# Value rows loaded in five transfers a pair with 96-key runs, and two table halves negated on VectorE

## The chip, the cores and the metric

The kernel runs on one core of one Trainium2 chip. The metric is the device time in microseconds (us) of one execution, as the median of several runs. The core has five instruction streams that matter here: TensorE (PE, with its weight loads shown as PEld), VectorE (DVE), ScalarE (ACT), GpSimd (POOL) and SyncE (SP). SP, ACT and POOL can each issue DMA transfers, and 16 DMA engines move the data.

## What is computed

Chunked attention, then a Fourier mix, a layer norm and a two-layer MLP. Shapes: q, k and v are (4 batches, 8 heads, 768, 64) in float32, with 8 memory keys and values for each head; x is (4, 768, 512); the MLP is 512 to 2048 to 512.

```
for c in range(24):                          # chunks of 32 queries
    keys  = 8 memory keys + k[32*c-16 : 32*c+40]    # 16 left, 32 own, 8 right, cut at the ends
    a     = softmax(q_c @ keys.T / 8)
    out_c = a @ values
x   = heads side by side
u   = x + real(fft(fft(x, axis=1), axis=2))
un  = (u - mean) / sqrt(var + 1e-6)
out = u + max(un @ w_ch1, 0) @ w_ch2
```

## The kernel before

**Pairs and tiles.** The 32 heads are taken as 16 pairs, n = 0 to 15, four pairs for each batch (`HP` = 4). The 768 positions of a head are cut into `NT` = 12 tiles of 64 queries (two chunks). For each tile, scores are computed with the keys on the partitions: partitions 0 to 7 hold the memory keys, 8 to 23 the 16 left keys, 24 to 87 the 64 own keys, 88 to 95 the 8 right keys. `OWN` is 24 and `KEYS` is 96. Neighbouring tiles overlap, so the value buffer `va` ([128 partitions, 2 heads, 12 tiles, 66], float32) holds each value row more than once; column 64 of a row is 1, so that the softmax's denominator comes out of the same product. There are four such buffers (`NV` = 4), so pair n uses buffer n % 4.

**Value loads** (`e_load_v`, lines 386 to 406). For one pair: one transfer for the own rows of tile 0 of both heads (line 399), and for each head one of left and own rows of tiles 1 to 11 (80 partitions x 11 tiles, line 392), one of right rows of tiles 0 to 10 (8 partitions x 11 tiles, also line 392), and one that repeats the 8 memory values for 12 tiles (line 405). That is seven transfers, whose pieces are rows of 64 floats, 256 bytes. All are issued by SP, except that in batch 0 the 80-row transfer of the second head is issued by ACT (`half == 1`).

**Edges.** The left rows of tile 0 and the right rows of tile 11 do not exist. They are set to 0 once for each buffer, with their column 64 (`e_edges`, lines 351 to 355, and `e_edge_ones`, lines 357 to 365), by GpSimd except for buffer 0. `e_masks` (lines 339 to 345) makes the bias `mbias` that takes out, for the first chunk of a tile, keys 64 to 95, and for the second chunk the keys ahead of its left context.

**Keys and products.** `e_kT` (line 450) spreads the turned keys over `kTb` with 88 columns for each tile (11 blocks of 8). `e_scores` (line 464) and `a_scores` make the scores `sc`; `e_exp` (line 475) and `a_exp` write `e1` on `KEYS` partitions; `e_values` (line 511, matmul at line 523) multiplies `e1[0:KEYS]` with `va[0:KEYS]` into `xa` (tiles 0 to 5) and `xo` (tiles 6 to 11); `e_norm` (line 527) divides.

**Fourier tables.** In batch 0 the sequence transform takes its rows in two halves (`g_rows`, line 719, matmul at line 729); the second half needs `odd`, the negative of one parity of the cosine and sine tables. `e_negatives` (line 1232, instruction at line 1234) makes it on GpSimd, two instructions on 128 x 579 float16.

**Order.** Each engine follows a list of task numbers written out by hand (`lists`, from line 1597). The planner (`Plan.order`) plays the lists through with a cost for each task, and from that decides in which overall order the instructions are emitted, which of two PSUM banks a task gets, and how many filler matmuls (`e_fill`, line 1040) PE runs where the planner has it idle in the first part of the kernel. Task 113 is the negation. It stands in GpSimd's list behind the q load of pair 2 and ahead of the last edge tasks and the q and k loads of pair 3 (tasks 88 and 89). A GpSimd copy of one value (`e_gate`, line 1121) reads a row of pair 3's second head; behind it in GpSimd's list stand the q and k loads of pairs 4 and 5 and the first two weight loads.

Of the kernel before, what the change touches and what calls it, by code (L numbers as in the profile page):

```python
# [16 lines left out]
CHUNK = 32  # L17
# [5 lines left out]
OWN = MEM0 + NMEM + LEFT  # L23
KEYS = OWN + 2 * CHUNK + RIGHT

# [183 lines left out]
def kernel(  # L209
# [129 lines left out]
    def e_masks():  # L339
        nc.gpsimd.memset(mbias, 0.0)  # L340
        nc.gpsimd.memset(mbias[64:96, 0:1], NEG)
        nc.gpsimd.affine_select(out=mbias[:, 1:2], in_=mbias[:, 1:2], compare_op=ALU.is_ge,
                                fill=NEG, base=-(OWN - LEFT + CHUNK), pattern=[[0, 1]],
                                channel_multiplier=1)
        nc.gpsimd.memset(mbias[MEM0:MEM0 + NMEM, 1:2], 0.0)
# [5 lines left out]
    def e_edges(i):  # L351
        v1, eng = va[i], nc.vector if i < 1 else nc.gpsimd
        eng.memset(v1[:, :, :, D:D + 1], 1.0)  # L353
        eng.memset(v1[0:32, :, 0, 0:D], 0.0)
        eng.memset(v1[64:96, :, NT - 1, 0:D], 0.0)

    def e_edge_ones(i):
        v1 = va[i]
        lo, hi = v1[0:32, :, 0, D:D + 1], v1[64:96, :, NT - 1, D:D + 1]
        nc.gpsimd.affine_select(out=lo, in_=lo, compare_op=ALU.is_ge, fill=0.0, base=-OWN,  # L360
                                pattern=[[0, 2], [0, 1]], channel_multiplier=1)
        nc.gpsimd.affine_select(out=hi, in_=hi, compare_op=ALU.is_ge, fill=0.0,
                                base=OWN + 63 - 64, pattern=[[0, 2], [0, 1]],
                                channel_multiplier=-1)
        nc.gpsimd.memset(v1[MEM0:MEM0 + NMEM, :, 0, D:D + 1], 1.0)
# [20 lines left out]
    def e_load_v(n, half=None):  # L386
# [3 lines left out]
        def run(p0, count, t0, nt, key, hh, by):  # L390
# [3 lines left out]
                                      ap=[[D, count], [64 * D, nt], [1, D]]))  # L394

        if half == 1:
            run(OWN - LEFT, LEFT + 64, 1, NT - 1, 64 - LEFT, 1, nc.scalar)
            return
        nc.sync.dma_start(v1[OWN:OWN + 64, :, 0, 0:D],
                          v[b, 2 * pr:2 * pr + 2, 0:64].rearrange("h p d -> p h d"))  # L400
        for hh in range(2):
            if half is None or hh == 0:
                run(OWN - LEFT, LEFT + 64, 1, NT - 1, 64 - LEFT, hh, nc.sync)
            run(OWN + 64, RIGHT, 0, NT - 1, 64, hh, nc.sync)
            nc.sync.dma_start(v1[MEM0:MEM0 + NMEM, hh, :, 0:D],
                              mem_v[b, 2 * pr + hh].unsqueeze(1).to_broadcast([NMEM, NT, D]))
# [43 lines left out]
    def e_kT(n, eng=None):  # L450
        if n >= TURNED * HP:
            win = LEFT + 64 + RIGHT
            nc.vector.tensor_copy(
# [4 lines left out]
        (eng or nc.scalar.copy)(  # L458
            strided(kTb[n % NKT], MEM0 + NMEM, [[P, NT], [RB, 11], [1, RB]]),
            strided(trk, 0, [[64 // RB, NT], [1, 11], [KP, RB]]))  # L460
        if n < 2 or n in JOINED:
# [49 lines left out]
    def e_values(n, g):  # L511
# [6 lines left out]
        for st in range(3):  # L518
            for hh in range(2):
                v1 = va[n % NV]  # L520
                for half in range(2):
                    t6 = 2 * st + half
                    nc.tensor.matmul(xa[64 * half:64 * half + 64, st, hh, 0:65],  # L523
                                     e1[0:KEYS, hh, t6, :], v1[0:KEYS, hh, 6 * g + t6, 0:65],
                                     start=True, stop=True)
# [706 lines left out]
    def e_negatives():  # L1232
        for i, tab in enumerate((cosS, sinS)):
            nc.gpsimd.tensor_scalar(odd[:, i], tab[:, 1], -1.0, None, ALU.mult)

# [22 lines left out]
    t_warm = add("ACT", 1.6, lambda: nc.scalar.activation(warm, zero, AFT.Exp), [t_late], rank=LATER)  # L1258
    t_neg = shared(add("POOL", 3.3, e_negatives, [t_sines], rank=100))
    t_rows = shared(add("POOL", 2.8, e_table_rows, [t_late, t_neg], rank=LATER))  # L1260
# [330 lines left out]
    for b in range(B):  # L1591
# [6 lines left out]
        "DVE": [  # L1598
# [18 lines left out]
        ],  # L1617
# [34 lines left out]
        "POOL": [  # L1652
# [4 lines left out]
        ],  # L1657
# [40 lines left out]
```

## Time and profile before

| | us |
|---|---|
| median of 3 runs | 272.72 |
| lowest, highest | 272.63, 278.22 |
| the profiled execution | 271.1 |
| its span in the profile | 269.4 |

The profiled execution's own time is 1.7 us above its span. TensorE's granted clock was 1.0 in it.

A row of a timeline gives the start in us, the duration in us, the engine, the line, the operation with what it writes and reads, the number of instructions merged, and in brackets how long the engine had been idle and what released it. A row of the chain of waits gives start, duration and what held the chain; "DMA" there is the time from a transfer's issue to its landing, "SPq" the issuing of a transfer on SP. A row of the DMA view gives a queue's packets, megabytes and the time of its packets as a share of 16 engines' time: q1 is SP's queue, q10 ACT's, and q0 ("software") GpSimd's. In the lists of groups the last numbers are total busy us and mean ns of one instruction.

### The profile page before, as it was taken

To read this page: it belongs to the slowest core of one execution; us is meant where nothing else is said; L and a number is where in the kernel's file an instruction comes from. 1 tells how busy PE (TensorE), PEld (TensorE's weight loads), DVE (VectorE), ACT (ScalarE), POOL (GpSimd) and SP (SyncE) were. 2 spreads that over 40 slices of the span, in tenths; PEclk is the share of its full clock that TensorE was granted. 3 is DMA by queue.
4 is the path that set the end of the run, shared out by engine and by line. 5 is a ranking of instruction groups with operands and counts; after the bars stand their busy time and mean duration, and the time that the engine had idled before them with its cause. 6 is when DMAs were issued, how large, how long until landed. Compare 5 with 4: busy or idle time off the path is not lost.

```text
span 269.4 us, 8363 instructions
## 1 busy us (share of the span) xinstructions
PE 260.8 (97%) x3469; PEld 215.8 (80%) x3469; DVE 202.7 (75%) x456; ACT 162.8 (60%) x318; POOL 89.6 (33%) x159
## 2 busy tenths in 40 slices
PE   6999899999999999999899999999999999999995
PEld 6556597888964778857798888888988988888884
DVE  6867488863379779999999989999887855354444
ACT  6757868899866279766742974726627171715150
POOL 7985463045120091564480550006006231000000
PEclk9999999999999999999999999999999999999999
DMA  6999999979998999989999974681913233334263
GB/s 102 206 180 191 211 195 200 213 126 195 197 241 169 130 218 175 126 222 206 197 218 161 159 169 88 165 130 19 238 20 82 61 77 80 89 61 108 56 166 92
DMA packets 116118, 40.00 MB, mean 148 GB/s; under 512 B 104560, under 2 KB 111472, under 8 KB 116080
## 3 DMA queue, kind: packets, MB, share of 16 engines
q1 hardware_dynamic: 90304, 22.64, 46.5%
q0 software_dynamic: 21472, 15.21, 34.8%
q10 hardware_dynamic: 4304, 1.62, 3.0%
q8 instruction: 27, 0.44, 0.7%
q14 instruction: 11, 0.09, 0.1%
HBM read 37.36 MB, written 13.37 MB: 188 GB/s over the span
## 4 chain that ended last, share of the span: by engine, by line
PE 73%; DVE 11%; DMA 8%; POOL 4%; issue 1%; SPq 1%; ACT 0%; POOLq 0%
PE ph L908 27%; PE pc L975 21%; PE pc L926 5%; PE ps L595 5%; DMA va<-in_v_dram 5%; DMA va<-in_mem_v_dram 3%; PE xa L523 3%; PE xo L523 3%; PE ps L729 2%; PE pm L768 2%; DVE st L843 1%; DVE xsb L534 1%; PE pm L789 1%; DVE xsb L817 1%; PE sc L494 1%
## 5 line engine op out<-in xcount | busy, mean ns | idle before, releaser
L908 PE MATMUL ph<-unT,w_sb 128*128 128x256 f16 x768 | 88.9, 273 | 0.2 <-DVE xsb L980 0.2
L917 ACT ACTIVATE hT<-ph 128x512 f16<-128x512 f32 x96 | 55.2, 600 | 51.6 <-PE pc L975 37.5
L908 PEld LDWEIGHTS <-w_sb 128*128 128x128 f16 x768 | 74.2, 98 | 9.7 <-issue 0.5
L975 PEld LDWEIGHTS <-hT 128*128 128x128 f16 x360 | 34.6, 98 | 4.5 <-DVE hT L963 0.2
L975 PE MATMUL pc<-w_sb,hT 128*128 128x256 f16 x288 | 36.6, 273 | 0.0
L980 DVE TENSOR_TENSOR xsb<-pc,xsb 128x256 f32<-128x256 f32 x64 | 26.1, 419 | 13.7 <-PE pc L975 12.8
L831 POOL TENSOR_TENSOR xsb<-mix,xr 128x512 f32<-128x512 f32 x9 | 12.3, 1384 | 42.3 <-ACT mix L825 24.4
L506 ACT ACTIVATE e<-sc,mbias 96x192 f32<-96x192 f32 (+1 forms) x48 | 19.0, 470 | 5.0 <-PE sc L494 5.0
L926 PE MATMUL pc<-w_sb,hT 128*128 128x512 f16 x96 | 21.7, 379 | 0.0
L481 ACT ACTIVATE e<-sc,mbias 96x384 f32<-96x384 f32 x32 | 17.0, 573 | 6.8 <-PE sc L471 6.8
L963 DVE TENSOR_TENSOR S<-hT 128x768 f16<-128x768 f16 (+1 forms) x18 | 7.6, 421 | 17.2 <-ACT hT L917 16.9
L857 ACT ACTIVATE un<-xsb,rs 128x512 f16<-128x512 f32 x18 | 14.4, 821 | 5.3 <-POOL rs L872 5.3
L975 PE MATMUL pc<-w_t,S 128*128 128x256 f16 x144 | 17.4, 273 | 0.0
L926 PEld LDWEIGHTS <-hT 128*128 128x128 f16 x96 | 9.1, 98 | 10.1
L843 DVE BATCH_NORM_STATS2 st<-xsb 128x6 f32<-128x512 f32 x24 | 16.3, 681 | 0.8 <-POOL xsb L831 0.6
L523 PE MATMUL xa<-va,e 96*64 96x65 f32 x384 | 14.9, 226 | 1.3 <-DMA va<-in_mem_v_dram 1.3
L523 PEld LDWEIGHTS xa<-va,e 96*64 96x64 f32 x384 | 12.6, 137 | 3.7 <-issue 2.9
L975 PEld LDWEIGHTS <-S 128*128 128x128 f16 x144 | 14.0, 98 | 1.6
L523 PE MATMUL xo<-va,e 96*64 96x65 f32 x384 | 14.1, 223 | 0.0
L1040 PE MATMUL idle<-dz 128*128 128x512 bf16 x46 | 12.9, 387 | 1.0 <-DVE va L353 1.0
L433 ACT COPY qT<-trq 128x768 bf16<-128x768 bf16 x12 | 9.6, 796 | 6.6 <-PE trq L415 6.4
L523 PEld LDWEIGHTS xo<-va,e 96*64 96x64 f32 x384 | 12.6, 138 | 0.4 <-ACT e L481 0.2
(192 smaller groups left out, 489.1 us busy)
## 6 DMA issues: line engine op xcount, KB each, us to landing
va<-in_v_dram SPq DMA_DIRECT2D x28, 220.0 KB
w_sb<-in_moe_w_ch_dram POOLq DMA_DIRECT2D x8, 512.0 KB, 9.0
out_dram<-xsb SPq DMA_DIRECT2D x12, 256.0 KB
qs<-in_q_dram POOLq DMA_DIRECT2D x12, 192.0 KB, 6.7
ks<-in_k_dram POOLq DMA_DIRECT2D x12, 192.0 KB, 6.6
x_rows<-xsb POOLq DMA_DIRECT2D x3, 768.0 KB, 5.1
xr<-x_back POOLq DMA_DIRECT2D x3, 768.0 KB, 5.7
out_rows<-xsb SPq DMA_DIRECT2D x9, 256.0 KB
```

The source lines that it names most:

```text
L481: nc.scalar.activation(e1[0:KEYS, :, :, ts(half, 32)], sc[0:KEYS, :, 0:6, ts(half, 32)], AFT.Exp, bias=mbias[0:KEYS, half:half + 1], scale ...
L506: nc.scalar.activation(to, src, AFT.Exp, bias=mbias[0:KEYS, half:half + 1], scale=1.0 / math.sqrt(D))
L523: nc.tensor.matmul(xa[64 * half:64 * half + 64, st, hh, 0:65], e1[0:KEYS, hh, t6, :], v1[0:KEYS, hh, 6 * g + t6, 0:65], start=True, stop=True)
L595: nc.tensor.matmul(out_[:, sp, :], part[:, ab, sp * 3 + st, c0:c1], tab[:, sp, st, :], start=(st == 0 and i == 0), stop=(st == 2 and i == 1))
L843: nc.vector.bn_stats(st6, xs[b][:, kt, :])
L857: nc.scalar.activation(un, xs[b][:, kt, :], AFT.Identity, bias=rs[:, 1:2], scale=rs[:, 0:1])
L908: nc.tensor.matmul(ph[:, k, :], w1_sb[:, dt, ts(HH * k + i, P)], unT_of[b, j][:, dt, :], start=(dt == 0), stop=(dt == NDT - 1))
L917: nc.scalar.activation(hT_of[b, j][:, :, i, :], ph, AFT.Relu, bias=0.0, scale=1.0 if (b, j) in FAST else -1.0)
L926: nc.tensor.matmul(pc_of[b, j, r], hT_of[b, j][:, k, i, ts(r, P)], w2_sb[:, HH * k + i, :], start=(i + k == 0), stop=(i + k == HH))
L975: nc.tensor.matmul(pc_of[key], a[:, i, :], w[:, i, :], start=(i == 0 and new), stop=(i == HH - 1), skip_group_check=not new)
L980: nc.vector.tensor_tensor(u, pc, u, ALU.add)
L1040: nc.tensor.matmul(fill_of[0], dz, strided(dz, 0, [[0, 4], [1, P]]), start=True, stop=True)
```

## The change

The keys of a tile are followed by 16 rows instead of 8 (`AFTER` = 16), so that `KEYS` grows from 96 to 104. Right rows then need no transfer of their own: left, own and following rows of a tile are one run of 96 consecutive keys. For each head that is one transfer of 96 partitions x 11 tiles, and tile 0 of both heads takes one of 80 rows; with the two of memory values a pair has five transfers. The run of tile 11 reads 16 rows into the next head, which the last tile's product leaves out (it uses `LAST` = 88 rows); only for the very last head, where there is no next, the run is split into two transfers. The mask takes out keys 64 to 103 for the first chunk and 96 to 103 for the second. The edge memsets and selects for tile 11 go. `e_kT` spreads 96 columns a tile instead of 88. Task 113 moves from GpSimd to VectorE, with a planned cost of 0.5 us instead of 3.3, behind task 69 (the norm of pair 1's second half) and ahead of task 116 (the first Fourier fold). The other numbers in the lists keep their order.

```diff
-KEYS = OWN + 2 * CHUNK + RIGHT
+AFTER = 2 * RIGHT
+LAST = OWN + 2 * CHUNK
+KEYS = LAST + AFTER
...
-        nc.gpsimd.memset(mbias[64:96, 0:1], NEG)
+        nc.gpsimd.memset(mbias[64:P, 0:1], NEG)
+        nc.gpsimd.memset(mbias[96:P, 1:2], NEG)
...
         eng.memset(v1[0:32, :, 0, 0:D], 0.0)
-        eng.memset(v1[64:96, :, NT - 1, 0:D], 0.0)
...
-        lo, hi = v1[0:32, :, 0, D:D + 1], v1[64:96, :, NT - 1, D:D + 1]
+        lo = v1[0:32, :, 0, D:D + 1]
...
-        nc.gpsimd.affine_select(out=hi, in_=hi, compare_op=ALU.is_ge, fill=0.0,
-                                base=OWN + 63 - 64, pattern=[[0, 2], [0, 1]],
-                                channel_multiplier=-1)
...
+        def rows(hh, by):
+            whole = (b, 2 * pr + hh) != (B - 1, H - 1)
+            run(OWN - LEFT, KEYS - OWN + LEFT, 1, NT - 2 + whole, 64 - LEFT, hh, by)
+            if not whole:
+                run(OWN - LEFT, LEFT + 64, NT - 1, 1, S - 64 - LEFT, hh, by)
+
         if half == 1:
-            run(OWN - LEFT, LEFT + 64, 1, NT - 1, 64 - LEFT, 1, nc.scalar)
+            rows(1, nc.scalar)
             return
-        nc.sync.dma_start(v1[OWN:OWN + 64, :, 0, 0:D],
-                          v[b, 2 * pr:2 * pr + 2, 0:64].rearrange("h p d -> p h d"))
+        nc.sync.dma_start(v1[OWN:KEYS, :, 0, 0:D],
+                          v[b, 2 * pr:2 * pr + 2, 0:64 + AFTER].rearrange("h p d -> p h d"))
         for hh in range(2):
             if half is None or hh == 0:
-                run(OWN - LEFT, LEFT + 64, 1, NT - 1, 64 - LEFT, hh, nc.sync)
-            run(OWN + 64, RIGHT, 0, NT - 1, 64, hh, nc.sync)
+                rows(hh, nc.sync)
...
-            strided(kTb[n % NKT], MEM0 + NMEM, [[P, NT], [RB, 11], [1, RB]]),
-            strided(trk, 0, [[64 // RB, NT], [1, 11], [KP, RB]]))
+            strided(kTb[n % NKT], MEM0 + NMEM, [[P, NT], [RB, 12], [1, RB]]),
+            strided(trk, 0, [[64 // RB, NT], [1, 12], [KP, RB]]))
...
+                    rows = LAST if 6 * g + t6 == NT - 1 else KEYS
                     nc.tensor.matmul(xa[64 * half:64 * half + 64, st, hh, 0:65],
-                                     e1[0:KEYS, hh, t6, :], v1[0:KEYS, hh, 6 * g + t6, 0:65],
+                                     e1[0:rows, hh, t6, :], v1[0:rows, hh, 6 * g + t6, 0:65],
...
-            nc.gpsimd.tensor_scalar(odd[:, i], tab[:, 1], -1.0, None, ALU.mult)
+            nc.vector.tensor_scalar(odd[:, i], tab[:, 1], -1.0, None, ALU.mult)
...
-    t_neg = shared(add("POOL", 3.3, e_negatives, [t_sines], rank=100))
+    t_neg = shared(add("DVE", 0.5, e_negatives, [t_sines], rank=100))
...
-            30, 69, 116, 31, 120, 115, 92, 119, 83, 87, 123, 100, 129, 134, 104, 132, 138, 137, 142, 141, 227,
+            69, 113, 116, 31, 120, 115, 92, 119, 83, 87, 123, 100, 129, 134, 104, 132, 138, 137, 142, 141, 227, 144,
...
-            36, 2, 11, 37, 55, 54, 13, 15, 18, 71, 9, 8, 19, 12, 70, 113, 10, 14, 88, 89, 32, 91, 208, 207,
+            36, 2, 11, 37, 55, 54, 13, 15, 18, 71, 9, 8, 19, 12, 70, 10, 14, 88, 89, 32, 91, 208, 207, 225, 224,
```

More of the change, by code (lines that the diff above doesn't have):

```diff
@@ L451, in e_kT @@
         if n >= TURNED * HP:
-            win = LEFT + 64 + RIGHT
+            win = LEFT + 64 + AFTER
             nc.vector.tensor_copy(
```

39 rows, old and new, of the table lists are left out of this document.

## The prediction, as made before the result was known

> **What bounds the kernel now.** I read the page first, then the chain of waits, then the stretch before 34 us in it, because there alone the chain is not on TensorE.
>
> ```profile
> PE 73%; DVE 11%; DMA 8%; POOL 4%; issue 1%; SPq 1%; ACT 0%; POOLq 0%
> ```
>
> TensorE holds 73% of the chain, so what counts is where it waits, and how much of its work is filler. Its waits after 33 us (us in all, times, longest):
>
> ```profile
> PE ps L595 <- ACT hT L917: 0.7, 1, 0.7
> PE pm L768 <- DVE up L757: 0.5, 1, 0.5
> PE ph L908 <- DVE xsb L980: 0.2, 1, 0.2
> ```
>
> Only 1.4 us in 236, and no transfer among them: a microsecond won on TensorE before 33 us should last to the end. The 8% of DMA lies before that. The chain there:
>
> ```profile
> 17.01 5.83 DMA va<-in_v_dram
> ...
> 22.85 0.27 SPq L392
> ...
> 23.16 9.32 DMA va<-in_mem_v_dram
> ```
>
> The last transfer of pair 3's values is issued at 23.16 and lands 9.32 us later; the value product of that pair has begun and stands still for it. On TensorE's timeline:
>
> ```profile
> 23.41 0.82 PE L1040 MATMUL idle<-dz 128*128 128x512 bf16 x3
> ...
> 30.95 0.34 PE L523 MATMUL xa<-va,e 96*64 96x65 f32 x4
> 32.62 0.80 PE L523 MATMUL xa<-va,e 96*64 96x65 f32 x20 [1.33 <-DMA va<-in_mem_v_dram]
> ...
> 34.46 0.92 PE L523 MATMUL xo<-va,e 96*64 96x65 f32 x24
> ```
>
> The undisturbed group takes 0.92; this one took from 30.95 to 32.62 + 0.80 = 33.42, so **the stall costs 33.42 - 30.95 - 0.92 = 1.55 us**.
>
> Why is that transfer late? Two things. First, SP issues late:
>
> ```profile
> 15.73 0.59 SPq L399 DMA_DIRECT2D va<-in_v_dram  x1
> 16.36 1.08 SPq L392 DMA_DIRECT2D va<-in_v_dram  x2
> 17.49 0.32 SPq L405 DMA_DIRECT2D va<-in_mem_v_dram  x1
> 17.96 0.27 SPq L392 DMA_DIRECT2D va<-in_v_dram  x1
> 18.28 0.31 SPq L405 DMA_DIRECT2D va<-in_mem_v_dram  x1
> 18.64 0.59 SPq L399 DMA_DIRECT2D va<-in_v_dram  x1
> 19.79 1.89 SPq L392 DMA_DIRECT2D va<-in_v_dram  x2
> 21.72 0.31 SPq L405 DMA_DIRECT2D va<-in_mem_v_dram  x1
> 22.85 0.27 SPq L392 DMA_DIRECT2D va<-in_v_dram  x1
> ```
>
> The chain hangs the one at 22.85 on the landing of the one of 17.01 (the second of the row of 16.36). Counting rows, it is the eighth after it, and buffers of different pairs are concerned. I read: a transfer from SP or ACT waits for the landing of the one eight places earlier, so eight are in flight, whatever their size. Second, GpSimd's loads then take the DMA engines. The DMA view of 20 to 24 us, then of 24 to 32 us:
>
> ```profile
> q1 hardware_dynamic: 1414, 0.35, 43.8%
> ```
> ```profile
> q0 software_dynamic: 882, 1.43, 101.4%
> q1 hardware_dynamic: 558, 0.13, 11.6%
> ```
>
> SP's queue falls from 1414 / 4 = 354 packets a us to 558 / 8 = 70. That flood begins behind GpSimd's gate, which waits for ACT's load of pair 3:
>
> ```profile
> 11.87 1.70 POOL L1234 TENSOR_SCALAR odd<-cosS 128x579 f16<-128x579 f16 x1
> 13.54 1.80 POOL L1234 TENSOR_SCALAR odd<-sinS 128x579 f16<-128x579 f16 x1
> ...
> 19.91 0.18 POOL L1121 COPY gate<-va 1x1 f32<-1x1 f32 x1 [0.38 <-DMA va<-in_v_dram]
> ```
>
> **The change, part by part.** *Transfers and packets.* A pair has 128 + 2 x (880 + 88 + 96) = 2256 pieces of 256 bytes before, and 160 + 2 x (1056 + 96) = 2464 after: 9% more. In batch 0, SP's share goes from 1376 to 1408, ACT's from 880 to 1056. But eight in flight are now 1.6 pairs instead of 1.1. Counting the new order, pair 2's first two wait for the end of pair 0 and the first transfer of pair 1 only, and the last transfer of pair 3 (memory values, second head) is the eighth after ACT's load of pair 3, the very one that opens the gate.
>
> *When pair 3 lands.* ACT's loads of pairs 1 to 3 have 3 x 176 = 528 more packets; at SP's lone rate of 354 a us that is 1.5 us, so the gate opens at about 19.9 + 1.5 = 21.4, and the flood reaches SP's queue at about 25.5 instead of 24. The last transfer is issued at about 21.4 too. Ahead of it stand at most pair 3's 1056-piece run and the other memory transfer: 1056 + 192 = 1248 packets, 3.5 us at 354. It lands near 25, and TensorE asks at 30.95. The slack is some 6 us, or 5.45 x 70 = 380 packets left over when the flood begins at 25.5. So the 1.55 us go. What is late next is the exponential of pair 3's second half, which its product reaches only behind twelve Fourier products (the 34.46 row above comes 34.46 - 33.42 = 1.04 after the first product's end), and then TensorE's own queue, which the three waits above show to be full: **-1.55 us**.
>
> By the Trainium skill, DMA: Bandwidth & Descriptors, section "Why a DMA increments its semaphore by 16 and not by 1", a transfer is spread over the largest number of engines up to 16 that divides its slowest dimension, which puts an 8-row transfer on 8 of the 16. By it the fuller engines would carry 2 x (55 + 11 + 12) + 8 = 164 pieces a pair before and 2 x (66 + 12) + 10 = 166 after, 1% more instead of 9%, and pair 3 would land earlier still; no row here names an engine.
>
> *The negation.* 1.70 + 1.80 = 3.5 us leave GpSimd. Behind it are the last edges and pair 3's q and k loads, which go some 3.5 us earlier; the gate does not, since it waits for a landing. VectorE gets two instructions of 579 float16 ahead of the first of these:
>
> ```profile
> 23.81 0.95 DVE L671 TENSOR_TENSOR half<-xsb 128x762 f32<-128x762 f32 x1
> ...
> 27.47 0.96 DVE L699 TENSOR_TENSOR lo<-half,hi 128x768 f16<-128x768 f32 x1 [1.04 <-ACT hi L695]
> ```
> ```profile
> L453 DVE COPY kTb<-kU 128x1056 bf16<-128x1056 bf16 x4 | 1.7, 420 | 0.0
> ```
> ```profile
> L671 DVE TENSOR_TENSOR half<-xsb 128x762 f32<-128x762 f32 x2 | 1.9, 949 | 0.1
> ```
>
> No row has this operation on VectorE. The low end is the 16-bit copy, 579 / 1056 x 420 = 0.23 each; the high end one float32 pass, 579 / 762 x 949 = 0.72 each. Nearest is the copy, one 16-bit source and no second operand: 0.5 for both, 1.4 at worst. Queued behind it are two folds, a small copy and the keys' constant columns, and then VectorE waits 1.04 us for ScalarE: 0.5 is hidden, of 1.4 some 0.4 would be left for whoever waits for that result. **0**, at worst +0.4.
>
> *Wider copies, more rows.* `e_kT` copies 12 columns of blocks instead of 11. The by-shape list has:
>
> ```profile
> L458 ACT COPY kTb<-trk 128x1056 bf16<-128x1056 bf16 x9 | 9.3, 1034 | 0.6 <-PE trk L415 0.6
> ```
> ```profile
> L415 PEld LDWEIGHTS <-qs 96*64 96x64 bf16 x192 | 5.1, 110 | 2.0 <-issue 1.6 <-DMA qs<-in_q_dram 0.4
> ...
> L415 PEld LDWEIGHTS <-ks 100*64 100x64 bf16 x192 | 5.0, 109 | 1.4 <-issue 1.3
> ```
>
> At most 1034 / 11 = 94 ns more for each of twelve, and TensorE's waits after 33 show the copies of later pairs in none: 0. The value product contracts 104 rows instead of 96: weight loads of 100 and 96 rows differ by 1 ns, so 0; the other bound is below, as a rival. The dropped edge memsets let pair 1's first load go a few tenths earlier, which the slack hides.
>
> *Filler.* The planner counted the negation as 3.3 us ahead of pair 3's loads. If it filled for these, as with the three fillers of 23.41 ahead of pair 3's turned q, up to 0.8 us of filler go; if it sees more competition among loads, as much may be added. I take 0.
>
> The sum: 271.1 - 1.55 = 269.5 for the profiled execution, and as the median of the runs lies 1.6 above that one, **272.72 - 1.55 = 271.2**.
>
> **The rivals.** *A: more filler goes.* -1.55 - 0.8 or somewhat more: 270.2. For it: fillers stand ahead of pair 3's q in the row of 23.41, and a filler runs whether the load has come or not; against it, no row shows what the planner saw. *B: the gain is given back.* VectorE carries 11% of the chain; if something fixed in time sets it (transposes and transfers on SP), the 0.7 us wait behind ScalarE and others grow again: 272.7, no change. The small waits after 33 speak against it. *C: slower.* The value loads are 9% more bytes and SP is still behind when the flood begins. It decides from 380 packets upward left at that time; if it begins as early as now and SP's order gains nothing, the 128 more packets of SP at 70 a us add 1.8 us to the stall: 272.72 + 1.8 = 274.5. For it: the second DMA view. Against: the gate itself now opens later, and SP's last transfer is issued with it. The Trainium skill, same page, section "Queues, rings and completion order", has each engine take turns between queues packet by packet, big against small; by that rule every packet added ahead of the end of pair 3 costs one big packet of GpSimd's queue, which is C, and the trace agrees as far as 558 small went beside 882 big ones. *D: the longer contraction costs in proportion*, 8 of 96, on both products of 16 pairs, 0.92 + 0.92 each: 16 x 1.84 x 8 / 96 = +2.5, so 272.72 - 1.55 + 2.5 = 273.7. The weight load rows speak against it.
>
> **Numbers.** Forecast 0.55, A 0.17, B 0.14, C 0.10, D 0.04. The forecast's own range is 270.6 to 271.8 (VectorE's 0.4, a few fillers either way). To leave out no more than 2 in 10, the range takes in most of A and of B and the near part of D: 269.7 to 273.1, with C and part of A outside. 2% of 272.72 is 5.5 us, about what a measurement of this kernel can tell from no change; no case reaches that by itself: faster 0.02, same 0.95, slower 0.03, the rest being several misfortunes at once.
>
> **What would show it.** Right: pair 3's last memory transfer lands before 30 us, no wait of TensorE for `va`; SP's line 399 of pair 2 is issued near 11 instead of 15.73; the gate copy comes after 20.5; the two negations on VectorE sum to 0.5 near 23.7, and the 1.04 us wait shrinks. Wrong: a TensorE wait for `va` at the same place or at pairs 1 or 2, a value product above 0.92, more filler matmuls at line 1040 than before, or new TensorE waits after 33 us.

## The result, and the profile after

| | before | after |
|---|---|---|
| median, us | 271.88 (22 runs) | 273.56 (22 runs) |
| lowest, highest | 269.56, 278.24 | 270.48, 275.95 |
| the profiled execution | 271.1 | 271.49 |
| its span | 269.4 | 269.8 |

The changed kernel is slower by a little: ratio 1.0082, 95% interval 1.0052 to 1.0111. That is within 2%, but on the other side of 1 than predicted, and 273.56 lies above the range. The ratios here and below leave out the runs more than 1.5% above the fastest of their kernel, so a ratio and two medians can differ.

The granted clock goes with much of the spread. The seven runs of the changed kernel at a mean clock of 0.998 to 1.0, called full clock below, took 270.5 to 272.2 us, 271.4 on average. The other 15 read 0.994 or 0.988; in profiles of such runs further down, the trace has 3.4 or 6.8 us at half clock. For the kernel before, 103 of the runs that stand beside the experiments have their clock on record: 60 were at 0.998 or above, from 269.5 us on, 270.6 on average. So at full clock the change costs some 0.8 us, an estimate from these two averages, and fewer of its runs stay there.

Share of the chain by engine, after (the row before stands at the head of the prediction):

```profile
PE 71%; DVE 8%; SPq 7%; DMA 7%; POOL 4%; ACT 2%; issue 1%; ACTq 0%; POOLq 0%
```

VectorE's share fell from 11% to 8% and SP's issuing rose from 1% to 7%: there are new waits on transfers. TensorE runs the same matmuls in the same order in both profiles, so the starts of the same matmul can be subtracted. Once the first pair's q is there, at 6.7 us, the difference is 0 until 17.27 us, then +1.14 at the turned keys of pair 2, -0.36 from pair 3's value product on, +0.32 from pair 5's value product (59.94 to 60.26), and +0.46 from 102 us. TensorE's timeline after, at these three places:

```profile
18.40 0.55 PE L419 MATMUL trk<-turn_b,ks 100*64 100x100 bf16 x16 [1.06 <-ACT qT L437]
...
32.09 0.92 PE L528 MATMUL xa<-va,e 104*64 104x65 f32 x24
...
60.26 0.80 PE L528 MATMUL xa<-va,e 104*64 104x65 f32 x20 [0.49 <-DMA va<-in_mem_v_dram]
```

The second row is the predicted gain: all 24 matmuls of pair 3's product in one piece of 0.92 us, where the row of before was broken for 1.33 us. The first and third rows are new waits. The chain of waits says where the first one comes from:

```profile
8.13 9.04 DMA va<-in_v_dram
17.17 0.02 issue
17.19 0.32 ACTq L391
17.51 0.04 issue
17.55 0.81 ACT qT L437
18.36 0.04 issue
18.40 0.55 PE trk L419 x16
```

SP's long run of pair 1, issued at 8.13, lands at 17.17. Until then ScalarE cannot issue its own load of pair 3, and behind that load in ScalarE's list stands the copy that TensorE needs. ScalarE's timeline after:

```profile
13.36 1.05 ACT L485 ACTIVATE e<-sc,mbias 104x384 f32<-104x384 f32 x2 [0.33 <-PE sc L475]
17.19 0.32 ACTq L391 DMA_DIRECT2D va<-in_v_dram  x1
17.55 0.80 ACT L437 COPY qT<-trq 128x768 bf16<-128x768 bf16 x1 [3.15 <-DMA va<-in_v_dram]
```

ScalarE stood 3.15 us. In the kernel before the same load was issued at 13.35, with no stand:

```profile
13.35 0.32 ACTq L392 DMA_DIRECT2D va<-in_v_dram  x1
...
14.22 0.79 ACT L433 COPY qT<-trq 128x768 bf16<-128x768 bf16 x1
```

The eighth transfer ahead of it was then pair 1's short first one. With five transfers a pair instead of seven, the eighth ahead is pair 1's long run.

SP's timeline after shows the intended part:

```profile
10.01 0.32 SPq L404 DMA_DIRECT2D va<-in_v_dram  x1
10.38 1.01 SPq L391 DMA_DIRECT2D va<-in_v_dram  x1
13.39 4.01 SPq L409 DMA_DIRECT2D va<-in_mem_v_dram  x2
17.68 0.32 SPq L404 DMA_DIRECT2D va<-in_v_dram  x1
...
21.52 0.64 SPq L409 DMA_DIRECT2D va<-in_mem_v_dram  x2
```

Pair 2's first transfer goes at 10.01 instead of 15.73, and pair 3's last at 21.84, to land at 27.27. GpSimd's and VectorE's timelines after, at the gate and the negations:

```profile
10.93 0.65 POOL L382 DMA_DIRECT2D qs<-in_q_dram  x1 [0.43 <-PE mps L1221]
11.58 0.63 POOL L382 DMA_DIRECT2D ks<-in_k_dram  x1
...
24.49 0.18 POOL L1126 COPY gate<-va 1x1 f32<-1x1 f32 x1 [10.79 <-DMA va<-in_v_dram]
```
```profile
24.77 0.31 DVE L1239 TENSOR_SCALAR odd<-cosS 128x579 f16<-128x579 f16 x1
24.99 0.31 DVE L1239 TENSOR_SCALAR odd<-sinS 128x579 f16<-128x579 f16 x1
```

The gate opens 4.58 us later than before. Pair 3's q and k loads go 5.8 us earlier than the 16.71 and 17.41 of before. Behind this are the moved negation and the dropped edge work; pair 2's q load goes at 8.79 instead of 11.14, in `loads_alone` below as well.

### The profile page after: what moved, and what is told of

Same layout as the page of the kernel before. It is cut to its first block, busy times and chain, and to the rows that moved or that the text cites. A ratio compares the mean times of both kernels' runs of the same rounds, so it can differ in the third digit from the quotient of the medians.

```text
span 269.8 us, 8305 instructions
## 1 busy us (share of the span) xinstructions
PE 261.6 (97%) x3469; PEld 216.4 (80%) x3469; DVE 202.6 (75%) x457; ACT 163.9 (61%) x318; POOL 84.2 (31%) x151
## 4 chain that ended last, share of the span: by engine, by line
PE 71%; DVE 8%; SPq 7%; DMA 7%; POOL 4%; ACT 2%; issue 1%; ACTq 0%; POOLq 0%
PE ph L913 25%; PE pc L980 21%; PE pc L931 5%; PE ps L600 5%; SPq L409 5%; PE xa L528 4%; DMA va<-in_v_dram 3%; DMA va<-in_mem_v_dram 3%; PE xo L528 3%; PE idle L1045 2%; SPq L391 1%; DVE st L848 1%; PE pm L794 1%; PE trk L419 1%; PE sc L475 1%
## 5 line engine op out<-in xcount | busy, mean ns | idle before, releaser
L510 ACT ACTIVATE e<-sc,mbias 104x192 f32<-104x192 f32 (+1 forms) x48 | 19.2, 483 | 4.9 <-PE sc L498 4.9
L485 ACT ACTIVATE e<-sc,mbias 104x384 f32<-104x384 f32 x32 | 17.2, 581 | 5.4 <-PE sc L475 5.4
L528 PE MATMUL xa<-va,e 104*64 104x65 f32 x384 | 14.9, 226 | 0.5 <-DMA va<-in_mem_v_dram 0.5
L528 PEld LDWEIGHTS xa<-va,e 104*64 104x64 f32 x384 | 12.6, 137 | 2.9 <-issue 1.3
L528 PE MATMUL xo<-va,e 104*64 104x65 f32 (+1 forms) x384 | 14.1, 223 | 0.0
L1045 PE MATMUL idle<-dz 128*128 128x512 bf16 x46 | 12.9, 387 | 1.0 <-DVE va L356 1.0
L528 PEld LDWEIGHTS xo<-va,e 104*64 104x64 f32 (+1 forms) x384 | 12.6, 138 | 0.4 <-ACT e L485 0.2
```

Of the source, the lines that this page charges most:

```text
L485: nc.scalar.activation(e1[0:KEYS, :, :, ts(half, 32)], sc[0:KEYS, :, 0:6, ts(half, 32)], AFT.Exp, bias=mbias[0:KEYS, half:half + 1], scale ...
L510: nc.scalar.activation(to, src, AFT.Exp, bias=mbias[0:KEYS, half:half + 1], scale=1.0 / math.sqrt(D))
L1045: nc.tensor.matmul(fill_of[0], dz, strided(dz, 0, [[0, 4], [1, P]]), start=True, stop=True)
```

## The experiments

The theory: ScalarE's stand makes TensorE wait, and a longer wait is followed by half clock. The rivals: the 9% more pieces cost the time, or the negation's move does.

**One part alone, and the kernel before again.** `loads_alone` is the changed kernel with the negation back on GpSimd, at its old place and cost, `neg_alone` the kernel before with only the negation moved.

```diff
-            nc.vector.tensor_scalar(odd[:, i], tab[:, 1], -1.0, None, ALU.mult)
+            nc.gpsimd.tensor_scalar(odd[:, i], tab[:, 1], -1.0, None, ALU.mult)
```

> The kernel before, once more, as the null of all the others: ratio 1.000. What is to be read is whether TensorE's stop of 1.3 us at pair 3's value product, which the first profile showed, stands in this profile too. If the stop is the same in each execution, a further profile shows 1.2 to 1.5 us at the same place. If the landing of pair 3's last transfer wanders, it shows something else, down to none, and the 1.55 us that the prediction counted were more than the kernel before loses as a rule.

> The five transfers alone: the negation is back on GpSimd, at its old place. Theory 1 in its narrow form: the long run of pair 1 lands late because pair 3's q and k loads now go out 5 us earlier and compete with it. Then that run lands near 15.7 as before, ScalarE stands until about 16 instead of 17.2, TensorE waits 0 to 0.3 us, and the time is 0.3% below the changed kernel's. Rival: the bigger transfers and the new rotation alone do it; then ScalarE stands until 16.8 or later and the ratio to before stays near 1.006 to 1.010.

> The negation alone, on VectorE, with seven transfers a pair as before. Both theories expect no wait of ScalarE for a value load, since the eighth transfer before pair 3's load is the short one of pair 1's first tile. If the earlier q and k loads hurt by themselves, pair 1's runs land 1 us later and TensorE shows a wait of 0.3 us or more before 25 us, ratio 1.002 to 1.004; if not, the ratio is 0.998 to 1.002.

TensorE's waits in `before_again` (272.87 us median, ratio 1.003, 0.9975 to 1.0085), `loads_alone` (273.28, ratio 1.0087, 1.0053 to 1.0122) and `neg_alone` (276.58, ratio 1.0076, 1.0 to 1.0151):

```profile
PE xa L523 <- DMA va<-in_mem_v_dram: 3.0, 1, 3.0
```
```profile
PE trk L419 <- ACT qT L437: 1.9, 1, 1.9
```
```profile
PE xa L523 <- DMA va<-in_mem_v_dram: 4.6, 1, 4.6
```

The transfers alone bring a ratio as large as the change's, with the wait at pair 2's turned keys. The negation alone leaves that place untouched and has a wait of 4.6 us at pair 3's values: with 3.5 us less to do, GpSimd issues pair 3's q load at 13.96 instead of 16.71. Its ratio rests on two of twelve runs and reaches down to 1.0, so it does not clear the negation: only one of its twelve runs was at full clock, against six of twelve with the transfers alone. Which of the two parts brings the changed kernel's half clock is not settled. In the kernel before the wait at pair 3's values was 1.33 us in the first profile (1.55 with the product broken in two) and is 3.0 in `before_again`, where half clock sets in at 35.17 us, during the wait. It is no fixed quantity.

**The kernel before, a third look.**

> The kernel before, one more look. If the 1.55 us wait at pair 3's values is a matter of the single execution, this profile shows another size: near 0 where the run takes 269.5 to 270.2, and more than 2 us where it takes over 273.

It took 271.96 us, and TensorE's timeline has, at pair 3's values:

```profile
31.51 0.92 PE L523 MATMUL xa<-va,e 96*64 96x65 f32 x24
```

There is no wait at all, though the gate opened at 19.90 as in the first profile and GpSimd's loads went behind it. So 1.33, 3.0 and 0 us stand in three profiles of one program. The run's time is not lower for it: between 145 and 163 us its TensorE goes from 0.58 us ahead of the first profile to 0.84 behind it, with waits of 0.6 and 0.4 us for VectorE among it. I expected a low time where the wait is near 0, and that did not hold.

**The changed kernel again.**

> The changed kernel as it is, run once more beside the others: 272 to 274. The wait of TensorE ahead of the turned keys at 17 to 18 us is there again, at 1 to 2 us; where it is near 2 us the granted clock is half for one stretch of 3.4 us that begins within 5 us of it, and the mean clock reads 0.994.

274.34 us median, ratio 1.0177 (1.0123 to 1.023). ScalarE's timeline, and the stretches of TensorE's time from 19 us on (busy time of each engine, then the granted clock, DMA share and GB/s):

```profile
17.56 0.32 ACTq L391 DMA_DIRECT2D va<-in_v_dram  x1
17.92 0.80 ACT L437 COPY qT<-trq 128x768 bf16<-128x768 bf16 x1 [3.53 <-DMA va<-in_v_dram]
```
```profile
19.00:21.00 2.00, 2.00 (x51) 1.46 (x46) 1.61 (x3) 1.50 (x4) 0.00 (x0) 0.84 1.29 244
21.00:24.50 3.50, 3.50 (x63) 2.18 (x60) 1.26 (x4) 1.28 (x3) 0.00 (x0) 0.60 1.18 150
24.50:27.00 2.50, 2.50 (x52) 1.44 (x48) 2.37 (x7) 1.23 (x2) 2.14 (x5) 1.00 0.98 137
```

The stand is 3.53 us here and TensorE's wait 1.43. At full or half rate, 0.84 over 2 us is 0.64 us at half, and 0.60 over 3.5 us is 2.8 us: together 3.4 us of half clock, beginning about 1.6 us after the wait ended. Half clock for 3.4 us costs at most 1.7 us, and TensorE's shift between 18.8 and 23.6 us grew from 1.50 to 2.88. The Trainium skill, TensorE: Matmul & The Clock Gate, section "Part 1: The HAM clock gate (the "warmup" mystery)", gives the clock two rates, decided over a free-running window of 3413 ns. By that rule a drop lasts whole windows, and the traces agree: the clock records have it at half for 3.41 us in `after_again`, `neg_alone` and `lb3_later`, 6.83 in `loads_alone` and `before_again`, and 10.24 in `before_gate` below.

**ScalarE's load moved.** `lb3_later` puts it one copy and one pair of exponentials later in ScalarE's list, `lb3_early` ahead, right behind the load of pair 1; `sp_takes` lets SP issue it (`e_load_v` issues the second head's run of pair 3 on `nc.sync`). Of the lists, only the part that differs is shown.

```diff
-72, 106, 107, 39, 108, 109, 47, 73, 59, 51, 63,
+72, 106, 107, 39, 108, 109, 47, 59, 51, 73, 63,      lb3_later
+72, 106, 107, 39, 73, 108, 109, 47, 59, 51, 63,      lb3_early
```

> The changed kernel with one thing moved: ScalarE issues its value load for pair 3 (task 73) behind the copy of pair 1's turned q and the second exponential of pair 0, not ahead of them. Theory 1: ScalarE's queue stands at that load because eight transfers may be in flight and the eighth before it is now pair 1's long run on SP, so that TensorE waits 1.06 us for the q copy. Then that wait goes to under 0.2 us, the first 30 us of TensorE are 0.9 to 1.1 us shorter, and the time is 0.3 to 0.5% below the changed kernel's. Rival: the time is lost elsewhere (later loads, a lower clock); then TensorE's wait goes and the time stays within 0.1% of the changed kernel's 1.008.

> Changed kernel, with ScalarE's load of pair 3 placed right behind its load of pair 1, where the eighth transfer before it is one of pair 0's memory values, long landed. If ScalarE's standing at that load is the loss: no stand of 3 us, the wait of 1.06 us ahead of the turned keys at 17.3 us is gone, the granted clock is 1.0 in most runs, and the time falls by 1 to 3 us, to about 270.5. Rival, the gate: it now opens when that early load lands, some 5 us earlier than 24.5, GpSimd's loads begin at about 20, and pair 3's remaining transfers crawl: then a TensorE wait for va of 1 us or more is back at pair 2 or 3 and the time stays near 273.

> Changed kernel, with the long run of pair 3's second head issued by SP instead of ScalarE, so that nothing of ScalarE stands behind a transfer after 12 us. If ScalarE's standing is the loss: the wait at 17.3 us gone, clock 1.0 in most runs, 270 to 271. If the loss is the transfers themselves (96 rows, 9% more pieces, late gate): the wait for va comes at pair 3 instead, since SP has one more transfer to wait for, and the time stays at 273 or above.

`lb3_later`: 273.5 us, ratio 1.0132 (1.0064 to 1.0199). `lb3_early`: 273.43, 1.0103 (1.0052 to 1.0153). `sp_takes`: 274.23, 1.0118 (1.0072 to 1.0164). ScalarE's timelines of the first two:

```profile
20.74 0.32 ACTq L391 DMA_DIRECT2D va<-in_v_dram  x1
21.10 1.05 ACT L485 ACTIVATE e<-sc,mbias 104x384 f32<-104x384 f32 x2 [3.42 <-PE xo L528]
```
```profile
10.06 4.32 ACTq L391 DMA_DIRECT2D va<-in_v_dram  x2
14.43 0.78 ACT L1235 ACTIVATE cosS<-yS,hpi_b 128x579 f16<-128x579 f32 x1 [3.59 <-issue]
```

Moved later, the load still meets pair 1's long run, which in that run landed only at about 20.7, and ScalarE stands 3.42 us ahead of an exponential; the bracket names a product done by 20.83, but the chain of waits has the load there. TensorE waits 1.5 us for VectorE at 18 us. Moved ahead, it need not wait for a landing, but issuing a third long run into ScalarE's queue took 3.96 us by itself, and TensorE waited 1.4 us for an exponential. Given to SP, ScalarE stands nowhere, and TensorE waits 1.1 us in all for the values of pairs 1 and 5, beside 0.5 us with no releaser shown at 18 us. Each time the first wait is gone and another has come, and the gain that was expected came in none: the lowest runs are 272.96, 271.38 and 272.02.

**The later load without the stand.** `lb3_late` moves the load behind two more pairs of exponentials; `late_gate` also lets the gate read pair 2's values. The planner answered with 59 fillers instead of 46, as the list by shape of `lb3_late` shows:

```profile
L1045 PE MATMUL idle<-dz 128*128 128x512 bf16 x59 | 15.7, 385 | 1.0 <-DVE va L356 1.0
```

`late_lean` and `late_lean2` therefore keep the changed kernel's own order and move this one load, behind task 67 and behind task 63.

```diff
...
+        order = plan.settled(lists)
+        load = next(t for t in order if t.get("no") == 73)
+        order.remove(load)
+        order.insert(1 + next(i for i, t in enumerate(order) if t.get("no") == 67), load)      late_lean
```

> Changed kernel, with ScalarE's load of pair 3 four exponentials and one copy later in its list, to be reached near 21.7 us, with the eighth transfer before it a short one of pair 1. If ScalarE's stand is what costs, it is gone (under 0.5 us), no TensorE wait of 1 us or more stands between 15 and 25 us, the clock is 1.0 in most runs and the fastest runs come down from 270.5 to 269.5 to 270. What is late next: the gate of GpSimd, at about 27 instead of 24.5, so 0.5 to 1 us at pair 3's turned keys or pair 5's values. If the total of the transfers is what costs, a wait of 1 us for va or qs comes in its place before 33 us and the median stays at 273 or above.

> As the run with the later load, and the gate of GpSimd reads pair 2's values (SP's long run) instead of pair 3's, so that it opens near 20 to 22 us. If the late gate is the rest of the loss: pair 5's wait for va goes, the end lies 0.5 us earlier than in the run with the later load, and the fastest runs are at 269 to 269.5. If the loads behind the gate then take the engines from pair 3's values: a wait of 1 us or more for va at pair 3, as in the kernel before.

> As the run with the later load, but every engine's order is the changed kernel's own, with its 46 fillers instead of 59; only ScalarE's load of pair 3 stands later, behind the exponentials of 20.6 us. If ScalarE's stand is the loss and the 13 fillers the rest: clock 1.0 in most runs, no TensorE wait at 17.3 us, 273.7 less 2.8 = 270.9 or below, median 270 to 271.5. If the transfers themselves cost: a wait for va or qs of 1 us or more between 20 and 35 us, and 272.5 or more.

> The same with the load two exponentials earlier, reached near 19.5 us, and the eighth transfer before it ScalarE's own load of pair 2, landed by then. The gate opens about 1 us earlier than in the run beside it: pair 5's wait is smaller. By the theory of the stand 270 to 271.5; by the rival (transfers) 272.5 or more.

`lb3_late`: 273.82 us, ratio 1.0133 (1.0085 to 1.0181), five of six runs at full clock. `late_gate`: 275.16, 1.019 (1.0126 to 1.0254). `late_lean`: 274.59, 1.0048 (1.0016 to 1.008). `late_lean2`: 272.02, 1.005 (1.0019 to 1.0081). TensorE's waits in `late_lean` and `late_lean2`:

```profile
PE xa L528 <- DMA va<-in_mem_v_dram: 3.5, 1, 3.5
...
PE xa L528 <- DMA va<-in_v_dram: 0.6, 1, 0.6
```
```profile
PE xa L528 <- DMA va<-in_v_dram: 1.8, 1, 1.8
```

No wait stands at the turned keys any more. The 13 added fillers (15.7 us of filler instead of 12.9) account for the 2.6 us by which `lb3_late` is behind at 59 us. But the full-clock runs of the two lean kernels begin at 271.3 and 271.1, no lower than the changed kernel's. TensorE now waits for the long runs themselves: 0.6 and 1.8 us at pair 1's values near 21 us, and 3.5 us at pair 5's in the first. The stand is thus only the first place at which the late landing of pair 1's transfers is felt.

**The rotation and the pieces, told apart.** `seven` cuts each memory transfer of batch 0 into two of four rows, the same pieces in seven transfers. `before_more` widens the short runs of the kernel before from 8 to 16 rows, which adds 176 pieces a pair that nothing reads. `narrow` is the changed kernel with 88-key runs (`AFTER = RIGHT`), 2272 pieces a pair.

```diff
-            run(OWN + 64, RIGHT, 0, NT - 1, 64, hh, nc.sync)
+            run(OWN + 64, 2 * RIGHT, 0, NT - 1, 64, hh, nc.sync)      before_more
...
-AFTER = 2 * RIGHT
+AFTER = RIGHT                                                         narrow
```

> Changed kernel, with each of the two memory transfers of a pair of batch 0 cut into two of four rows: the same pieces of 256 bytes in seven transfers instead of five. The eighth transfer before ScalarE's load of pair 3 is then pair 1's short first one again, as in the kernel before. If the rotation of eight is the cause: ScalarE does not stand at that load for more than 0.5 us, the wait of 1.06 us at 17.3 us is gone, SP is late again (pair 2's first transfer near 15 instead of 10.0) and TensorE waits 1 us or more at pair 3's values. If the wider runs are the cause: the wait at 17.3 us stays at about 1 us or more.

> The kernel before, with 16 rows instead of 8 in each short run: 176 more pieces of 256 bytes a pair (8%), in the same seven transfers in the same rotation; the added rows are read by nothing. If the added pieces are what costs the changed kernel its last 1 us (about 1248 packets of the first six pairs at some 700 to 800 packets a us of all queues): the fastest runs go from 269.5 to 270.5 or above. If the rotation and ScalarE's stand are all of it: 269.5 to 270 in the fastest runs, as the kernel before.

> The changed kernel with 88-key runs, 8 rows behind the chunk instead of 16: five transfers a pair as in the change, with 144 + 2 x (968 + 96) = 2272 pieces, nearly as many as before, and with key copies and 96 rows in the products as before. If the pieces are what costs: the fastest runs come down from 270.5 to 269.5 or 270. If the rotation is: 270.5 to 271.5, with ScalarE standing 3 us at its load of pair 3 as in the changed kernel. If both, in between, with a shorter stand.

`before_more`: 272.15 us, ratio 0.9993 (0.9941 to 1.0046); its full-clock runs begin at 270.31, beside 269.51 of the kernel before, and average 271.0 as those do. So 8% more pieces in the short runs cost nothing that shows. `narrow`: 277.12 us, ratio 1.02 (1.0144 to 1.0256), all six runs at 276.8 or above and none at full clock; in its profile 6.83 us are at half clock. Its waits and ScalarE's timeline:

```profile
PE trk L419 <- ACT qT L437: 3.7, 1, 3.7
```
```profile
20.77 0.33 ACTq L391 DMA_DIRECT2D va<-in_v_dram  x1
21.14 0.80 ACT L437 COPY qT<-trq 128x768 bf16<-128x768 bf16 x1 [5.81 <-DMA va<-in_v_dram]
```

With 8% fewer pieces than the change, and the rotation of the change, the loss is the largest of all the kernels with five transfers. In the four profiles that have this rotation and ScalarE's load in its place, the issue of that load (0.02 us behind the landing of pair 1's long run in the chain above), the stand and TensorE's wait go together:

| | issued at | ScalarE stood | TensorE waited |
|---|---|---|---|
| after | 17.19 | 3.15 | 1.06 |
| after_again | 17.56 | 3.53 | 1.43 |
| loads_alone | 18.66 | 3.99 | 1.9 |
| narrow | 20.77 | 5.81 | 3.7 |

In the profile of `narrow` the 88-row run of pair 1 landed 3.6 us later than the 96-row run in that of the change. A rule of the Trainium skill, DMA: Bandwidth & Descriptors, section "Why a DMA increments its semaphore by 16 and not by 1", would make it slower: a transfer runs on the largest number of engines up to 16 that divides its slowest dimension. By that rule 88 rows take 11 engines and 96 take 16. No row here names the engine of a piece, and these profiles do not show that the rows did it: in `lb3_later` the 96-row run landed at 20.72, as late as the 88-row one at 20.75. Why `narrow` is the slowest of these stays open.

`seven`: 274.05 us, ratio 1.0152 (1.0121 to 1.0182). ScalarE's timeline, then SP's:

```profile
13.66 1.54 ACTq L391 DMA_DIRECT2D va<-in_v_dram  x1
...
15.24 0.80 ACT L439 COPY qT<-trq 128x768 bf16<-128x768 bf16 x1 [0.58 <-issue]
```
```profile
9.58 3.27 SPq L411 DMA_DIRECT2D va<-in_mem_v_dram  x4
19.61 0.32 SPq L404 DMA_DIRECT2D va<-in_v_dram  x1
```

ScalarE's load goes at 13.66 again and the copy behind it stands 0.58 us instead of 3.15, so the rotation is the cause of the stand. The rest of that expectation failed: TensorE's wait at the turned keys was 0.7 us with no releaser shown, pair 3's values were in time, and pair 5's were late by 3.9 us, with half clock setting in during that wait.

SP's second row bears on why pair 1's long run lands late. Pair 2's first transfer waited there for that run, which landed at 19.60, later than the 17.17 of the change, though nothing of pair 2 had gone out on SP beside it. In the six profiles of the kernel before and its variants, with 80 rows, the run landed between 15.39 and 16.84; in the eleven with 96 rows, `seven` among them, between 16.88 and 20.72. Common to the eleven are the wider run and pair 2's earlier q load, and no run tells these two apart.

**The gate.** `before_gate` is the kernel before, with the gate reading SP's long run of pair 3 in place of ScalarE's.

```diff
-                nc.gpsimd.tensor_copy(gate[64:65], va[n % NV][64:65, 1, NT - 1, 0:1])
+                nc.gpsimd.tensor_copy(gate[64:65], va[n % NV][64:65, 0, NT - 1, 0:1])
```

> The kernel before, with GpSimd's gate reading SP's long run of pair 3 instead of ScalarE's, so that its loads begin some 3 us later (gate near 23 instead of 19.9). If pair 3's wait at 31 us comes from these loads beside SP's last transfers: the wait is 0.3 us or less, full-clock runs stay at 269.5 to 270.5, and fewer runs than half are above 273, so that the median is below 270.5: faster than both. If the later loads then come too late: a wait of 0.5 us or more at pair 5's values near 60 us, and the median stays at 271 or above.

278.09 us, ratio 1.0227 (1.0149 to 1.0304). The gate on GpSimd's timeline, and TensorE's waits:

```profile
26.29 0.21 POOL L1121 COPY gate<-va 1x1 f32<-1x1 f32 x1 [6.65 <-DMA va<-in_v_dram]
```
```profile
PE xa L523 <- DMA va<-in_mem_v_dram: 5.8, 2, 4.7
```

With the gate 6.4 us later, there is no wait at pair 3, with the seven transfers of before in their order. Both waits of the row stand at pair 5's values near 60 us, half clock sets in during them, and none of the six runs was at full clock. So a late gate costs at pair 5. That it is what removed the wait at pair 3 is not shown, since `before_third` has none either, with the gate at 19.90. The changed kernel's gate is late by 4.58 us, and its wait of 0.49 us at pair 5 may be of this kind; `seven`, with the gate at 22.45, waits 3.9 us there, so the gate is not all of it.

## Why the prediction was wrong

**The step that failed** is "So the 1.55 us go. What is late next is the exponential of pair 3's second half". They went in the profile. But what was late next was not that exponential: it lay 14 us earlier, at pair 2's turned keys, and two faults made me miss what the change would cost.

First, the rule of eight in flight was right, but I counted it only for some of SP's transfers. The same count for ScalarE's load of pair 3 gives pair 1's long run instead of its short first transfer. That queue carries copies and exponentials as well, so a wait there is a wait of TensorE: +1.14 us in the profile. No term of the sum and no rival had it; the list of what would prove me wrong named a wait for `va` at pairs 1 or 2, which is where the lean kernels have it, and new waits of TensorE after 33 us, of which pair 5's is one. One count that I did make was wrong as well: I put pair 3's last transfer behind the landing of ScalarE's load of pair 3. In the trace it went at 21.84, just behind the landing at 21.50 of ScalarE's load of pair 1, and what waited for the load of pair 3 was a transfer of pair 4, at 24.37. What came out at pair 3 was as forecast all the same: none of the eleven profiles with five transfers has a wait at its values. And pair 1's long run landed at 17.17 instead of 15.71, which I had not asked about; `seven` speaks against pair 2's earlier transfers on SP as the reason, and the reason stays open.

Second, "272.72 - 1.55 = 271.2" took the wait of one execution off a median over many. Three profiles of before have waits of 1.33, 3.0 and 0 us there. Full-clock runs of before begin at 269.5, which is 271.1 less 1.55: it may be that in the best runs there was nothing to win, though none of these was profiled. What the change adds, 1.14 and at pair 5 another 0.68, would come on top of that: 269.5 + 1.8 = 271.3, and the full-clock runs of the change average 271.4. The rest of the way to the median of 273.56 goes with the half clock of 15 of the 22 runs, which the prediction did not have at all.

**The gate** was put at 21.4 and came at 24.49. The 19.9 + 1.5 assumed that ScalarE's load of pair 3 is issued where it was; it was 3.84 us later. It is the same fault, and it set the q and k loads of pairs 4 and 5 late, which may be behind the +0.68 us at pair 5.

**The 70 packets a us** came back, but too late to matter for pair 3. The DMA view of the changed kernel, of 24 to 28 us and then of 28 to 32 us:

```profile
q1 hardware_dynamic: 2435, 0.61, 105.3%
q0 software_dynamic: 74, 0.07, 11.3%
```
```profile
q0 software_dynamic: 628, 0.61, 104.1%
q1 hardware_dynamic: 426, 0.10, 21.0%
```

SP's queue moved 609 packets a us ahead of GpSimd's loads and 106 beside them, of which the last two us had 145, or 73 a us. Rival C had that rate right. What it had wrong is that SP would still be behind: pair 3's last transfer landed at 27.27. That GpSimd's loads are what delays pair 3's last values in the kernel before is not shown: in `before_third` they came at the same time (917 packets of GpSimd's between 24 and 32 us, 543 of SP's) and TensorE did not wait.

**The negation** costs VectorE what was said: 24.77 to 25.30 is 0.53 us for both, hidden. It was costed at nothing in all, though the prediction itself said that pair 3's q and k loads go 3.5 us earlier; in `neg_alone` there were 4.6 us of waiting at pair 3's values, and eleven of twelve runs were below full clock, so that 0 had no ground. The prediction also let the dropped edge work move pair 1's first load alone; it moved pair 2's q load by more than 2 us.

**Right** were the wider copies and the contraction of 104 rows; from the list by shape:

```profile
L462 ACT COPY kTb<-trk 128x1152 bf16<-128x1152 bf16 x9 | 10.0, 1114 | 0.6 <-PE trk L419 0.6
L528 PE MATMUL xa<-va,e 104*64 104x65 f32 x384 | 14.9, 226 | 0.5 <-DMA va<-in_mem_v_dram 0.5
```

And before:

```profile
L523 PE MATMUL xa<-va,e 96*64 96x65 f32 x384 | 14.9, 226 | 1.3 <-DMA va<-in_mem_v_dram 1.3
```

80 ns more for a copy, with the same 0.6 us of idle time ahead of them, and 226 ns for a product as before. Rival D is out. The fillers stayed at 46, so A is out too. The outcome lies between B and C: the gain is given back, and somewhat more, by the mechanism of neither and earlier.

**What stays open.** Every profile with five transfers has a wait of TensorE of more than 0.5 us ahead of 34 us that the first profile of before does not have, except `lb3_late`, which has 13 more fillers; no version here beats the kernel before. What makes the transfers of one program land microseconds apart from run to run is not known. And in each of the eleven profiles with half clock it set in during a TensorE wait of 1.4 us or more or within 1.6 us of its end. But `lb3_early` waited 1.4 us and stayed at full clock, and waits of 1.69 and 1.93 us at 5 to 7 us, in `loads_alone` and `lb3_later`, were followed by full clock until past 20 us. That the wait causes it, and from what length, was not shown.

## What to carry to other kernels

When several transfers share a fixed number of places in flight, changing the count of transfers changes which landing each later issue waits for; count it for every issuing engine, and first for those whose list also holds compute. Work that is dropped or moved off an engine also moves the loads that it issues behind, so give those a place in the sum. And a wait on a transfer read from one profile is a sample: look at several executions before its length is taken off a median.

## What the runs showed of the hardware

An engine can stand at the issue itself, with no landing to wait for: ScalarE's third run of 1056 pieces took 3.96 us to issue at 10.4 us (`lb3_early`), where 0.32 is usual. One transfer can land microseconds apart in kernels that differ little around it: pair 1's run of 1056 pieces, issued at 8.1 us, landed between 16.88 us (`late_lean`) and 20.72 (`lb3_later`) in the eleven profiles that have it. And the clock falls to half for 3.4 to 10.2 us, during a TensorE wait or within 1.6 us of its end, which costs up to 1.7 us for each 3.4: in `after_again` about as much as the wait of 1.43 us ahead of it.
